# Third weight chunk loaded before the first gathers, half tile first in the last expert, two search waits lengthened: a retention and mixture-of-experts kernel on Trainium2

## The chip, the cores and the metric

The kernel runs on one core of one Trainium2 chip. The metric is device time in microseconds (us) of one execution; the medians below are over three executions. The engines of the core are TensorE (PE in the rows; its weight loads are PEld), VectorE (DVE), ScalarE (ACT), GpSimd (POOL) and SyncE (SP, which here only issues transfers). Each engine runs its own list of instructions in order, and waits on semaphores for the others.

## The reference

The first half is a retention layer: 8 batches, 8 heads, 576 positions, 64 elements a head. The second half is a mixture of 8 experts over the 4,608 tokens that result, with a strict routing: all (token, expert) scores are sorted, and a token goes to the best expert that still has one of its 576 places.

```python
scores = scale * np.matmul(q, k.transpose(0, 1, 3, 2))
ret = scores * Dmat[None, :, :, :]          # gamma**(i-j) where i >= j, else 0
x = np.matmul(ret, v)                       # -> N=4608 rows of D=512
logits = x @ w_gate                         # 4608 x 8
for idx in np.argsort(-logits.flatten()):
    tok, e = idx // E, idx % E
    if assigned[tok] >= 0 or counts[e] >= cap: continue
    assigned[tok] = e; counts[e] += 1
for e in range(E):
    h = np.maximum(x[assigned == e] @ w1[e], 0.0)      # 576x512 @ 512x1024
    out[assigned == e] = h @ w2[e]                     # 576x1024 @ 1024x512
```

All arrays are float32 in and out.

## The kernel before

**Stages.** `attention` (until about 140 us of the profile) streams 16 units of q, k and v through TensorE, writes the rows x to DRAM (`xd`) and forms the logits. Then the routing finds the experts one after the other: phase p finds the expert that fills up first among those left (a search over the bits of the scores, `search_first` for p = 0, `search` after that), its members (`members`), their row numbers (`listing`), and takes them out of the scores (`leave`). Phase 0 runs alone, from about 145 to 162 us, beside the last rows of x. Phases 1 to 7 are laid between the matrix products of the experts found before.

**One expert.** `l1` makes 16 tiles of the hidden layer (f = 0 to 7, each in two column groups s of 256 and 320 tokens), each from 12 products: every operand is split in a high and a low part (`xh`, `xl`, `w1h`, `w1l`), and three of the four combinations are multiplied. `l2` makes five tiles of the output, t = 0 to 3 with 128 tokens from 24 products each, t = 4 with the last 64 tokens from 16 products (it packs high and low parts beside each other, so that its two halves have to be added at the end). An expert has 192 + 112 = 304 products.

**Weights.** Each expert has eight chunks of 512 KB (four of w1, four of w2). `dma_pump` loads them on SP's queue into one of four `raw` buffers, and never more than `state['most']` in all until that is raised. `conv` turns one chunk into its high part (ACT, L946) and its low part: ACT writes the negated high part (L951) and a transfer issued by POOL adds the raw values (L952). For the first two chunks the low part of one is made by DVE (L949).

**The first expert.** When the first list is ready, `gather(0)` has POOL issue five indirect transfers of 128 rows (64 in the last) (L983). PE runs 25 empty products (`warm(25)`, L1175), then transposes the gathered rows (`pt`, L1015); ACT copies the high part `xh` out (L1017), DVE the low part `xl` (L1018). A tiny transfer `spacer2` on SP (L1144) waits for the third gather, so that SP's next weight loads start after it. In `l1` the first eight tiles are f = 0 to 3 with s = 0, then f = 0 to 3 with s = 1; the transpositions for j = 2, 3, 4 stand between tiles i = 2 to 4. With e == 0, f < 2 the order within a tile is all xh·w1h, then xh·w1l, then xl·w1h.

**What sets the order.** All of it is recorded in the program's order. A planner without knowledge of the chip (`Mixer`) lets a phase give up control with `yield (ns for DVE, ns for PE)`, and `mix.adv(ns)` after each group of products adds model time; when the model time of the yield has passed, the phase's next matmuls (L353 for the counts of a search step, L421 and L422 for the members, L459 and L462 for the list) are put behind the products recorded so far. From phase 2 on the model times of DVE are multiplied by 1.2 or 1.35. A larger number in a yield so puts the following PE instructions, and all that the phase does later, behind more products. On the chip each of those matmuls waits for DVE's result, and stands in line in front of the next product.

**The end.** After each `l2` tile ACT copies it to SBUF (L1109; L1111 and DVE's L1112 for t = 4), and POOL issues an indirect transfer to the output (L1069).

Of the kernel before, what the change touches and what calls it, by code (L numbers as in the profile page):

```python
# [15 lines left out]
AF = mybir.ActivationFunctionType  # L16
# [4 lines left out]
N, DM, E, FF = 4608, 512, 8, 1024  # L21
# [60 lines left out]
def rest(it):  # L82
    for _ in it:
        pass

class Route:
# [305 lines left out]
    def members(s, p):  # L392

        nc, V, pool, ps = s.nc, s.nc.vector, s.pool, s.ps
        mem = pool.tile([128, 2, 36], F32, name="mem")
        ba = pool.tile([128, 36], F32, name="ba")
        if p == E - 1:
            w = pool.tile([128, 8], F32, name="w8")
            V.tensor_scalar(w, s.nr, -10000.0, None, op0=ALU.is_ge)
            V.tensor_tensor(w, w, s.dec, op=ALU.mult)  # L400
            s.pick(w)
            V.tensor_scalar(ba, s.acc, s.mx, None, op0=ALU.is_equal)
            V.scalar_tensor_tensor(mem[:, 0], s.m, -1.0e38, ba, op0=ALU.is_ge, op1=ALU.add)
            V.memset(mem[:, 1], 0.0)
        else:
            V.scalar_tensor_tensor(mem, s.mx8[:, None, :].to_broadcast([128, 2, 36]), s.mx, s.ge, op0=ALU.is_equal, op1=ALU.mult)
            if p:
                V.scalar_tensor_tensor(mem[:, 0], s.acc, s.mx, mem[:, 0], op0=ALU.is_equal, op1=ALU.add)
        sc = pool.tile([128, 2, 36], BF16, name="sc")
        fl = lambda a: a.rearrange("p a b -> p (a b)")  # L410
        with nc.allow_low_precision(reason="counts up to 72"):
            V.tensor_tensor_scan(fl(sc), fl(mem), fl(mem), 0.0, op0=ALU.add, op1=ALU.bypass)

        sm = pool.tile([128, 2, 36], F32, name="sm")
        V.tensor_tensor(sm, sc, mem, op=ALU.mult)
        V.scalar_tensor_tensor(sm[:, 0], sm[:, 0], -1.0 - HALF, sm[:, 1], op0=ALU.add, op1=ALU.add)
        if not p:
            s.idle(6)
        yield (3000 if 0 < p < E - 1 else 1550 if not p else 1900), 125
        po = ps.tile([128, 2], F32, name="r")  # L420
        nc.tensor.matmul(po, s.tri, sc[:, :, 35], start=True, stop=False, skip_group_check=True)  # L421
        nc.tensor.matmul(po[:, 1:2], s.up, sc[:, 0, 35:36], start=False, stop=True, skip_group_check=True)  # L422
        q = pool.tile([128, 36], F32, name="pq")
        V.scalar_tensor_tensor(sm[:, 1], mem[:, 0], po[:, 0:1], sm[:, 0], op0=ALU.mult, op1=ALU.add)
        V.scalar_tensor_tensor(q, mem[:, 1], po[:, 1:2], sm[:, 1], op0=ALU.mult, op1=ALU.add)
        s.q, s.mem = q, mem
# [70 lines left out]
    def leave(s, p):  # L497

        nc, V, pool, ps = s.nc, s.nc.vector, s.pool, s.ps
        if p == 0:  # L500
            s.taken()
        e = pool.tile([128, 8], F32, name="eb")
        a = pool.tile([128, 36], F32, name="gone")
        V.tensor_scalar(e, s.es, -2*BIG, BIG, op0=ALU.mult, op1=ALU.add)
        V.scalar_tensor_tensor(a, s.q, CAP - HALF, s.mem[:, 1], op0=ALU.is_lt, op1=ALU.mult)
        V.tensor_tensor(s.Lg, s.Lg, e[:, None, :].to_broadcast([128, 36, 8]), op=ALU.min)
        V.tensor_tensor(a, a, s.gt, op=ALU.add)
        if p == 0:
            V.tensor_scalar(s.cap, a, -2*BIG, BIG, op0=ALU.mult, op1=ALU.add)
            V.tensor_tensor(s.acc, s.gt, s.mx8, op=ALU.mult)  # L510
        else:
            V.tensor_scalar(a, a, -2*BIG, BIG, op0=ALU.mult, op1=ALU.add)
            V.tensor_tensor(s.gt, s.gt, s.mx8, op=ALU.mult)
            V.tensor_tensor(s.cap, s.cap, a, op=ALU.min)
            V.tensor_tensor(s.acc, s.acc, s.gt, op=ALU.add)
        if p == 0:
            rest(s.best(capped=True))

            def after():
                cn = ps.tile([128, 8], F32, name="r")  # L520
                nc.tensor.matmul(cn, s.ones, s.n8, start=True, stop=True)
                s.room(cn)
            s.after = after
            yield 3800, 0
        else:
            rest(s.best(capped=True))
            yield (5000 if p == 1 else 4300), 0

def attention(tc, nc, P, qk, vk, cst_d, wg_d, rf, xd, Lg, raw):
    NC = cst_d.shape[1]  # L530
# [51 lines left out]
    def qscale(u, *parts):  # L582

        q, e = LD[u, 'q'], ex[:, u % HP]
        for a, b in parts:
            n = 128 if a < 1024 else 64
            x = q[:, a:b].rearrange("p (c i) -> p c i", i=n)
            nc.gpsimd.tensor_tensor(x, x, e[:, None, :n].to_broadcast([128, (b-a)//n, n]), op=ALU.mult)  # L588
# [205 lines left out]
    def fills(u, g):  # L794
        for f, a in fill.get(2*u + g, []): f(*a)

    P['warm'](7)
    qscale(0, (0, 512))
    kscale(0, 0, 8)
    scores(0, 0)  # L800
# [92 lines left out]
def moe(tc, nc, P, R, xd, w1_d, w2_d, out, mix):  # L893
    V, A, T = nc.vector, nc.scalar, nc.tensor
    ident, warm = P['ident'], P['warm']
# [1 line left out]
    ready = lambda k: len(found) > k  # L897
    regs, XG, quarters, parts = {}, {}, {}, {}
    xq = xd.rearrange("n (a c) -> (n a) c", a=4)
    state = dict(dma=0, conv=0, most=2, listing=-1)  # L900
    RAW, W1, W2, XH, XL = {}, {}, {}, {}, {}
    scat, lows = [], []
    spacer, spacer2 = [P['c'].tile([1, 1], F32, name=f"spacer{i}") for i in range(2)]
# [118 lines left out]
    def l1(e, tr):  # L1022

        hb = P['w'].tile([128, 8, 1152], F32R, name="hb", bufs=1)
        order = [(f, s) for f in range(8) for s in range(2)]
        if e == 0:
            order[:8] = [(f, s) for s in range(2) for f in range(4)]
        for i, (f, s) in enumerate(order):
            wh, wl = [w.rearrange("p (f d m) -> p f d m", f=2, d=4)[:, f % 2] for w in W1[e, f // 2]]
            if i == 0 and e >= PIECES:  # L1030
                for _ in tr:
                    pass
            if i == 0 and e:
                next(tr, None)
                next(tr, None)
            elif e == 0 and i in (2, 3):
                next(tr, None)
            elif i == (1 if e else 4):
                for _ in tr:
                    pass  # L1040
            xh, xl = XH[e], XL[e]
            c, n = ((slice(0, 256), 256), (slice(256, 576), 320))[s]

            ps = P['pp'].tile([128, n], F32, name="ph", tag="y" if f in (2, 5) else f"h{s}", bufs=2)
            terms = [(w[:, d], x[:, d, c]) for d in range(4) for w, x in ((wh, xh), (wh, xl), (wl, xh))]
            if e == 0 and f < 2:
                terms = terms[0::3] + terms[2::3] + terms[1::3]
            elif i in (2, 3) and e == 0:
                terms = terms[0::3] + terms[1::3] + terms[2::3]
            for k, (w, x) in enumerate(terms):  # L1050
                T.matmul(ps, w, x, start=(k == 0), stop=(k == 11))  # L1051
                if k % 3 == 2:
                    mix.adv(320 + 80*s, e == 0 and i < 3)
                    gather(e + 1)
            A.activation(hb[:, f, c], ps, AF.Relu)  # L1055
            for a, b in ((0, 256),) if s == 0 else ((0, 256), (256, 320)):
                to = (640 if a == 0 else 64) + 256*s
                V.scalar_tensor_tensor(hb[:, f, to+a:to+b], ps[:, a:b], 0.0, hb[:, f, 256*s+a:256*s+b].bitcast(F32),  # L1058
                                       op0=ALU.max, op1=ALU.subtract)
            mix.vec(340 + 140*s)  # L1060
            if e == 0 and i == 4:
                state['most'] = 8*E
            if i in ((2, 4, 7, 10) if e else (3, 5, 7, 9, 11, 13)):
                conv()
        return hb

# [8 lines left out]
    def l2(e, hb):  # L1075
# [1 line left out]
        late = []  # L1077
        want = 4*(e + 1 < E)
        wait = 0
        for t in range(5):  # L1080
            n = 128 if t < 4 else 64
            ps = P['pp'].tile([128, DM], F32, name="py", tag="y", bufs=2)
            c = slice(128*t, 128*t+n)
# [21 lines left out]
                    tr = transposes(e + 1)  # L1105
                next(tr, None)
            y = P['w'].tile([128, DM], F32, name="yt", bufs=3)
            if t < 4:
                A.activation(y, ps, AF.Copy)  # L1109
            else:  # L1110
                A.activation(y[:n], ps[n:], AF.Copy)  # L1111
                V.tensor_tensor(y[:n], y[:n], ps[:n], op=ALU.add)  # L1112
# [13 lines left out]
    def run():  # L1126
        mix.drain(lambda: 0 in regs)
        dma_pump()
        mix.drain(lambda: ready(0))
        conv(True)  # L1130
        conv()
        gather(0)
        lows.pop(0)()
        mix.step()
        warm(25)
        tr = transposes(0)
        next(tr)
        warm(4)
        next(tr)
        lows.pop(0)()  # L1140
        mix.step()
        warm(2)

        nc.sync.dma_start(spacer2, XG[0][0:1, 2, 0:1])  # L1144
        state['most'] = 4
        dma_pump()
        for e in range(E):
            tr = l2(e, l1(e, tr))
# [73 lines left out]
```

## Time and profile before

| | |
|---|---|
| three executions | 620.79, 623.42, 626.26 us; median 623.42 |
| the profiled execution | 625.75 us; span of the trace 623.6 us; 2.15 us lie around it |
| PE busy | 600.7 us, 96% |
| DVE, ACT, POOL busy | 66%, 44%, 40% |
[...]

All rows count microseconds from the start of the span. The time of an execution is the span and about 2 us more. The profiled execution is near the slowest of the three others.

### The profile page before, as it was taken

Reading aid. Unit: us, or ns where it says so; the run is one execution under the profiler, and the core shown is the slowest. Engines: PE = TensorE matmul, PEld = TensorE weight load, DVE = VectorE, ACT = ScalarE, POOL = GpSimd, SP = SyncE. Lnnn points to the kernel's source line nnn. Section 1 sums busy time; section 2 is a strip of 40 time slices with the busy share of each in tenths; the row PEclk is TensorE's granted clock in tenths of the full one; section 3 lists DMA queues with packets and bytes.
Section 4 is the critical chain, followed back from the end, with each engine's and each line's share of the span. In section 5 each row is a group of like instructions: output and inputs, shape, how many; then the busy total and the mean of one; then the engine's idle time right before and its main releaser. Section 6 shows DMA issues by size and latency. Waiting matters only on the chain.

```text
span 623.6 us, 14775 instructions
## 1 busy us (share of the span) xinstructions
PE 600.7 (96%) x5722; PEld 518.1 (83%) x5722; DVE 410.6 (66%) x1488; ACT 271.6 (44%) x465; POOL 248.2 (40%) x295
## 2 busy tenths in 40 slices
PE   7899999998989999999999999999999999999995
PEld 5788888875579779988987897799789889989983
DVE  4556788888868888887885877689478733322200
ACT  2244433333347355461652447155526445554410
POOL 4886665500302172061243242224313877832111
PEclk8899999999989999999999999999999999999998
DMA  9999899854768589787789399659937897994501
GB/s 330 408 369 401 280 370 316 261 140 137 192 180 194 174 221 264 186 207 236 156 224 246 94 229 227 201 111 231 247 114 174 200 245 169 259 249 124 102 35 42
DMA packets 53496, 133.22 MB, mean 214 GB/s; under 512 B 7410, under 2 KB 22642, under 8 KB 53426
## 3 DMA queue, kind: packets, MB, share of 16 engines
q0 software_dynamic: 15376, 51.92, 38.0%
q1 hardware_dynamic: 37906, 80.10, 38.0%
q8 instruction: 45, 0.74, 0.5%
q10 hardware_dynamic: 144, 0.26, 0.1%
q14 instruction: 25, 0.20, 0.1%
HBM read 80.35 MB, written 18.87 MB: 159 GB/s over the span
## 4 chain that ended last, share of the span: by engine, by line
PE 74%; DVE 9%; issue 6%; DMA 6%; POOL 2%; ACT 1%; SPq 1%; POOLq 0%; DVEq 0%
PE ph L1051 28%; PE py L1092 28%; PE sc L603 4%; PE px L647 3%; DMA xg<-xd,idx 2%; PE pS L624 2%; PE px L638 2%; PE pT L679 1%; DMA raw<-in_w 1%; PE r L353 1%; PE pt L1015 1%; DVE am L612 1%; DMA qin<-in_qk 1%; DVE cst L544 1%; DMA nin<-in_vk 1%
## 5 line engine op out<-in xcount | busy, mean ns | idle before, releaser
L1092 PE MATMUL py<-w2h,hb 128*128 128x512 f32 x576 | 187.3, 397 | 0.0
L1051 PE MATMUL ph<-xh,w1h 128*128 128x320 f32 (+1 forms) x512 | 151.7, 302 | 3.2 <-ACT xh L1017 3.2
L1051 PE MATMUL ph<-xh,w1l 128*128 128x320 f32 (+1 forms) x512 | 149.2, 297 | 0.0
L1051 PE MATMUL ph<-xl,w1h 128*128 128x320 f32 (+1 forms) x512 | 149.0, 297 | 0.0
L1092 PE MATMUL py<-w2l,hb 128*128 128x512 f32 (+1 forms) x320 | 125.3, 392 | 0.0
L1092 PEld LDWEIGHTS py<-w2h,hb 128*128 128x128 f32 x576 | 104.5, 188 | 21.7
L1051 PEld LDWEIGHTS ph<-xh,w1h 128*128 128x128 f32 x512 | 96.4, 191 | 4.4 <-ACT xh L1017 3.8
L1055 ACT ACTIVATE hb<-ph 128x256 fp32r<-128x256 f32 (+1 forms) x128 | 51.9, 408 | 105.1 <-PE ph L1051 96.3
L1051 PEld LDWEIGHTS ph<-xl,w1h 128*128 128x128 f32 x512 | 96.4, 191 | 0.3
L1051 PEld LDWEIGHTS ph<-xh,w1l 128*128 128x128 f32 x512 | 96.4, 191 | 0.0
L1058 DVE SCALAR_TENSOR_TENSOR hb<-ph,hb 128x256 fp32r<-128x256 f32 (+1 forms) x192 | 58.0, 352 | 46.2 <-ACT hb L1055 39.4
L1069 POOL DMA_INDIRECT out_y<-yt,idx x40 | 40.5, 1013 | 105.7 <-ACT yt L1109 70.5
L1092 PEld LDWEIGHTS py<-w2l,hb 128*128 128x128 f32 (+1 forms) x320 | 56.7, 177 | 12.9
L952 POOL DMA_DIRECT2D w2l<-raw x32 | 29.4, 919 | 87.2 <-ACT w2l L951 48.2
L612 DVE TENSOR_TENSOR am<-sc,cst 128x1024 f32<-128x1024 f32 x32 | 39.1, 1223 | 33.1 <-PE sc L603 33.0
L588 POOL TENSOR_TENSOR qin<-qin,cst 128x512 f32<-128x512 f32 (+1 forms) x48 | 48.3, 1034 | 31.2 <-DMA qin<-in_qk 27.3
L1109 ACT ACTIVATE yt<-py 128x512 f32<-128x512 f32 x32 | 19.2, 599 | 93.6 <-PE py L1092 70.0
L983 POOL DMA_INDIRECT xg<-xd,idx x30 | 30.2, 1008 | 71.9 <-DMA raw<-in_w 37.0
L627 ACT ACTIVATE st<-pS,cst 128x128 f32<-128x128 f32 x64 | 23.5, 368 | 79.9 <-PE pS L624 79.9
L952 POOL DMA_DIRECT2D w1l<-raw x31 | 29.0, 959 | 49.0 <-ACT w1l L951 32.5
L603 PE MATMUL sc<-qin,kin 64*128 64x128 f32 x512 | 38.8, 293 | 3.7 <-DVE am L612 1.9
L971 POOL DMA_INDIRECT xg<-xd,quarter x36 | 35.6, 989 | 12.8 <-issue 9.4
(191 smaller groups left out, 939.0 us busy)
## 6 DMA issues: line engine op xcount, KB each, us to landing
raw<-in_w SPq DMA_DIRECT2D x56, 512.0 KB
w2l<-raw POOLq DMA_DIRECT2D x32, 512.0 KB
w1l<-raw POOLq DMA_DIRECT2D x31, 512.0 KB
qin<-in_qk SPq DMA_DIRECT2D x14, 576.0 KB
kin<-in_qk SPq DMA_DIRECT2D x14, 576.0 KB
vin<-in_vk SPq DMA_DIRECT2D x14, 576.0 KB
nin<-in_vk SPq DMA_DIRECT2D x14, 512.0 KB
xd<-raw SPq DMA_DIRECT2D x36, 128.0 KB
```

Source lines behind the costliest of these rows:

```text
L588: nc.gpsimd.tensor_tensor(x, x, e[:, None, :n].to_broadcast([128, (b-a)//n, n]), op=ALU.mult)
L603: nc.tensor.matmul(t[:, h, 128*j:128*j+128], blk(k, 4*g+j)[r], blk(q, 4*g+j)[r], start=(j == 0), stop=True, skip_group_check=True)
L612: nc.vector.tensor_tensor(a, SC[u, g].rearrange("p h (j q) -> p h j q", q=128), m1[:, u % HP, :, None, :].to_broadcast([128, 2, 4, 128]), ...
L627: nc.scalar.activation(s, p, AF.Copy, scale=ss[:, u % HP, c:c+1])
L952: add = lambda: nc.gpsimd.dma_start(lo, raw, accum_op=ALU.add)
L971: nc.gpsimd.indirect_dma_start(out=t[:, k, :], out_offset=None, in_=xq[:, :], in_offset=bass.IndirectOffsetOnAxis(ap=quarters[e][:, v:v+1] ...
L983: nc.gpsimd.indirect_dma_start(out=xg[:n, j, :], out_offset=None, in_=xd[:, :], in_offset=bass.IndirectOffsetOnAxis(ap=found[e][:n, j:j+1] ...
L1051: T.matmul(ps, w, x, start=(k == 0), stop=(k == 11))
L1055: A.activation(hb[:, f, c], ps, AF.Relu)
L1058: V.scalar_tensor_tensor(hb[:, f, to+a:to+b], ps[:, a:b], 0.0, hb[:, f, 256*s+a:256*s+b].bitcast(F32), op0=ALU.max, op1=ALU.subtract)
L1069: st = nc.gpsimd.indirect_dma_start(out=out[:, :], out_offset=bass.IndirectOffsetOnAxis(ap=found[e][:n, t:t+1], axis=0), in_=y[:n], in_off ...
L1092: T.matmul(ps[:m], a, w, start=(k == 0), stop=(k == last), skip_group_check=True)
```

## The change

There are five edits. (1) `most` starts at 3, so that three weight chunks are loaded ahead of the gathers, and the third is converted in `run`, behind the second transposition, no longer inside `l1` at tile i = 3. (2) In the last expert (`e + 1 == E`) the half tile t = 4 is made first, and tile 3 last. (3) The copy of that last tile is split: 256 columns by ACT, 256 by DVE. (4) The yield of `members` for p = 1 goes from 3000 to 3500, and that of `leave` for p = 2 from 4300 to 5000 (times 1.2 in the planner). (5) At the very start PE runs 12 empty products where it ran 7.

```diff
-        yield (3000 if 0 < p < E - 1 else 1550 if not p else 1900), 125
+        yield (3500 if p == 1 else 3000 if 1 < p < E - 1 else 1550 if not p else 1900), 125
...
-            yield (5000 if p == 1 else 4300), 0
+            yield (5000 if p < 3 else 4300), 0
...
-    P['warm'](7)
+    P['warm'](12)
...
-    state = dict(dma=0, conv=0, most=2, listing=-1)
+    state = dict(dma=0, conv=0, most=3, listing=-1)
...
-            if i in ((2, 4, 7, 10) if e else (3, 5, 7, 9, 11, 13)):
+            if i in ((2, 4, 7, 10) if e else (5, 7, 9, 11, 13)):
                 conv()
...
-        for t in range(5):
+        for t in range(5) if e + 1 < E else (4, 0, 1, 2, 3):
...
-            if t < 4:
+            if t == 3 and e + 1 == E:
+                A.activation(y[:, :256], ps[:, :256], AF.Copy)
+                V.tensor_copy(y[:, 256:], ps[:, 256:])
+            elif t < 4:
                 A.activation(y, ps, AF.Copy)
...
         next(tr)
         lows.pop(0)()
+        conv()
         mix.step()
         warm(2)
```

ACT's list at the first expert, from the first two transposed row groups on, before (xh is the high part of the rows, hb the hidden layer; L946 and L951 convert a weight chunk):

```order
L951 ACTIVATE w1l<-raw 128x1024
L1017 ACTIVATE xh<-pt 128x4x128 x2
L1055 ACTIVATE hb<-ph 128x256 x2
L1017 ACTIVATE xh<-pt 128x4x128
L1055 ACTIVATE hb<-ph 128x256
L1017 ACTIVATE xh<-pt 128x4x128
L1055 ACTIVATE hb<-ph 128x256
L946 ACTIVATE w1h<-raw 128x1024
L951 ACTIVATE w1l<-raw 128x1024
L1017 ACTIVATE xh<-pt 128x4x64
```

and with the change:

```order
L951 ACTIVATE w1l<-raw 128x1024
L1017 ACTIVATE xh<-pt 128x4x128 x2
L946 ACTIVATE w1h<-raw 128x1024
L951 ACTIVATE w1l<-raw 128x1024
L1055 ACTIVATE hb<-ph 128x256 x2
L1017 ACTIVATE xh<-pt 128x4x128
L1055 ACTIVATE hb<-ph 128x256
L1017 ACTIVATE xh<-pt 128x4x128
L1055 ACTIVATE hb<-ph 128x256
L1017 ACTIVATE xh<-pt 128x4x64
```

The conversion of the third chunk no longer stands between the fourth hidden tile and the copy of the last transposed rows (128x4x64).

DVE's list at the same place, which is the same in both kernels; L357 to L348 are a step of the search of phase 1, xl is the low part of the last transposed rows, and the waits are in brackets:

```order
L357 SCALAR_TENSOR_TENSOR cs<-room,r 32x8 [waits PE_49]
L359 TENSOR_TENSOR cs<-cs,r 32x8 [waits DVE_49] x2
L361 TENSOR_TENSOR f<-r,cs 32x8 [waits DVE_49]
L361 TENSOR_TENSOR f<-r,cs 32x8 x3
L367 TENSOR_REDUCE mq<-f 128x1 [waits DVE_49]
L368 STREAM_TRANSPOSE tc<-mq 128x32 [waits DVE_49]
L369 TENSOR_REDUCE j<-tc 128x1 [waits DVE_49]
L337 TENSOR_SCALAR v<-u,j 128x72 [waits DVE_49]
L177 TENSOR_TENSOR G<-ct,v 128x1152 [waits DVE_49]
L348 TENSOR_TENSOR u<-v,D 128x36
L1058 SCALAR_TENSOR_TENSOR hb<-ph,hb 128x256 [waits Activation_49]
L1018 TENSOR_TENSOR xl<-pt,xh 128x4x64 [waits Activation_49]
```

Nothing moved here: the last low part stands behind the whole search step.

The end of the program, before: ACT's last copies, then DVE's last addition (DMASW names are earlier transfers of POOL):

```order
L1109 ACTIVATE yt<-py 128x512 [waits DMASW4_49,PE_49,Activation_49]
L1111 ACTIVATE yt<-py 64x512 [waits DMASW5_49,PE_49,Activation_49]
L1112 TENSOR_TENSOR yt<-yt,py 64x512 [waits DMASW5_49,DMASW6_49,DMASW1_49,Activation_49]
```

and with the change (L1114 and L1115 are the half tile, now the first of the five; L1109 and L1110 are the split copy):

```order
L1114 ACTIVATE yt<-py 64x512 [waits DMASW5_49,PE_49,Activation_49]
L1112 ACTIVATE yt<-py 128x512 [waits DMASW4_49,DVE_49,PE_49]
L1109 ACTIVATE yt<-py 128x256 [waits DMASW5_49,PE_49,Activation_49]
L1115 TENSOR_TENSOR yt<-yt,py 64x512 [waits DMASW5_49,Activation_49]
L1110 COPY yt<-py 128x256 [waits DMASW5_49,DMASW6_49,DMASW1_49,Activation_49]
```

Of the two halves of the last copy, ACT's waits for PE, and DVE's waits for ACT.

## Rows read from the trace of the kernel before

**Rows 1.** Page, part 1: busy time of each engine, share, instructions.

```profile
PE 600.7 (96%) x5722; PEld 518.1 (83%) x5722; DVE 410.6 (66%) x1488; ACT 271.6 (44%) x465; POOL 248.2 (40%) x295
```

**Rows 2.** Waits of PE: line waiting, releaser, us in total, times, longest.

```profile
PE ph L1051 <- ACT xh L1017: 3.2, 2, 3.0
...
PE sc L603 <- POOL qin L588: 1.7, 1, 1.7
```

**Rows 3.** Timeline, 172 to 183 us: start, duration, instruction, count, idle before.

```profile
175.01 0.14 DVE L357 SCALAR_TENSOR_TENSOR cs<-room,r 32x8 f32<-32x8 f32 x1
...
175.48 0.50 PE L1015 MATMUL pt<-ident,xg 64*128 64x64 f32 x4
...
176.68 1.06 ACT L946 ACTIVATE w1h<-raw 128x1024 fp32r<-128x1024 f32 x1 [0.70 <-DMA raw<-in_w]
...
178.17 0.42 DVE L1058 SCALAR_TENSOR_TENSOR hb<-ph,hb 128x256 fp32r<-128x256 f32 x1
178.58 0.36 ACT L1017 ACTIVATE xh<-pt 128x256 fp32r<-128x256 f32 x1
...
178.98 0.42 DVE L1018 TENSOR_TENSOR xl<-pt,xh 128x256 fp32r<-128x256 f32 x1 [0.39 <-ACT xh L1017]
179.00 1.44 PE L1051 MATMUL ph<-xh,w1h 128*128 128x320 f32 x4 [3.02 <-ACT xh L1017]
...
182.37 0.75 PE L1051 MATMUL ph<-xh,w1h 128*128 128x320 f32 x4
```

**Rows 4.** Stretches: us, busy time by engine, PEclk, DMA share, GB/s.

```profile
175.00:178.96 3.96, 0.98 (x9) 0.74 (x7) 3.25 (x15) 2.66 (x4) 0.00 (x0) 1.00 0.81 236
178.96:182.37 3.41, 3.37 (x13) 3.37 (x13) 0.42 (x1) 0.00 (x0) 0.99 (x1) 0.50 0.99 302
```

**Rows 5.** Stretches of 1 us before the first gathers move data.

```profile
160.00:161.00 1.00, 1.00 (x6) 0.44 (x5) 0.89 (x6) 0.00 (x0) 0.00 (x0) 1.00 0.95 381
...
162.00:163.00 1.00, 1.00 (x6) 0.49 (x5) 0.60 (x1) 0.93 (x2) 0.97 (x1) 1.00 0.00 0
```

**Rows 6.** Timeline, 157 to 168 us: SP's weight loads, ACT's second transposed copy.

```profile
157.08 0.89 SPq L932 DMA_DIRECT2D raw<-in_w  x2
...
167.60 0.60 ACT L1017 ACTIVATE xh<-pt 128x512 fp32r<-128x512 f32 x1 [0.92 <-PE r L521]
```

**Rows 7.** Timeline, the first 18 us.

```profile
1.48 3.17 PE L1175 MATMUL warm<-full 128*128 128x512 bf16 x7 [1.48 <-DVE full L1161]
...
14.77 1.69 POOL L588 TENSOR_TENSOR qin<-qin,cst 128x512 f32<-128x512 f32 x2 [1.67 <-DMA qin<-in_qk]
...
17.51 0.45 PE L624 MATMUL pS<-vin,ks 128*64 128x64 f32 x8 [2.07 <-POOL ks L593]
```

**Rows 8.** Timeline, 285 to 290 us: search of phase 3 at the half tile of the second expert.

```profile
286.49 0.39 PE L353 MATMUL r<-oh,G 128*128 128x32 bf16 x9
...
289.19 0.46 DVE L177 TENSOR_TENSOR G<-ct,v 128x576 bf16<-128x576 bf16 x1
...
289.71 0.39 PE L353 MATMUL r<-oh,G 128*128 128x32 bf16 x9 [0.41 <-DVE G L177]
```

**Rows 9.** Timeline, PE, 319 to 324 us: second transposition for the fourth expert.

```profile
321.61 0.53 PE L1015 MATMUL pt<-ident,xg 128*128 128x128 f32 x4 [0.23 <-DMA xg<-xd,idx]
```

**Rows 10.** Timeline, the last 12 us.

```profile
612.46 0.60 ACT L1109 ACTIVATE yt<-py 128x512 f32<-128x512 f32 x1 [4.89 <-PE py L1092]
...
613.34 0.97 POOL L1069 DMA_INDIRECT out_y<-yt,idx  x1 [4.24 <-ACT yt L1109]
...
615.68 0.40 PE L1092 MATMUL py<-w2l,hb 128*64 128x512 f32 x1
616.17 0.59 ACT L1111 ACTIVATE yt<-py 64x512 f32<-64x512 f32 x1 [3.11 <-PE py L1092]
616.79 0.68 DVE L1112 TENSOR_TENSOR yt<-yt,py 64x512 f32<-64x512 f32 x1 [25.14 <-ACT yt L1111]
617.75 0.90 POOL L1069 DMA_INDIRECT out_y<-yt,idx  x1 [3.35 <-DVE yt L1112]
```

## The prediction, before the changed kernel was run

> **What bounds the kernel now.** I read the page's busy shares first. TensorE is busy for 600.7 of 623.6 us [rows 1], so all idle time of PE together is 23 us. About 7.5 of them lie behind its last product (616.08 to the end), so no edit that leaves the products alone can win much. The second view is the list of PE's waits: the only large one is 3.0 us for `xh`, the high part of gathered rows [rows 2]. The third is the timeline around it [rows 3]. PE ends the last transposition of the first expert at 175.98 (175.48 + 0.50) and starts the next tile at 179.00. Between them ACT stands at a weight conversion: it waits for the third chunk until 176.68, converts it in two passes, and only then copies the transposed rows (178.58 to 178.94). [...]
>
> **The third chunk, step by step.** The edit takes the conversion out of that place on ACT and puts it behind the second transposed copy, which ends at 168.20 [rows 6]. There it takes about 2.1 us (two passes of 1.06 [rows 3]), to 170.3. The first tile's twelve products start about 168.2 and take at most 0.14 each, so its copy comes some 0.4 us late; nobody waits for it, since DVE is in a search step and PE's next tiles have banks of their own. The third load goes out behind the two of 157.08 [rows 6]. It moves 0.52 MB, which at the 381 GB/s of the stretch from 160 takes 1.4 us, and from 162 to 163 the transfer engines carry nothing, while POOL is still issuing the first gather [rows 5]. So I price it at nothing, with the whole 1.4 us as the upper end.
>
> The last transposed copy then follows PE at once: 175.98 + 0.06 + 0.36 gives 176.4, and PE starts at 176.5 instead of 179.00. But what is late next is on DVE. Its list has not moved: the low part `xl` stands behind a whole search step that began at 175.01 and behind a hidden tile that ends at 178.59 (178.17 + 0.42); before, it waited another 0.39 for ACT. It will run from 178.6 to 179.0 [rows 3]. Eight of the tile's products need no `xl`: 8 x 0.14 brings PE to 177.6, there it waits 1.4 us, and the last four end at 179.6. Before, the tile ended at 182.37 [rows 3]. So the three microseconds are not all won: of 3.02 idle 1.9 remain, in pieces of 0.5 and 1.4. What is won depends on the clock. If it stays at its full level, the gain is 182.37 - 179.6 = **2.7 us**. If it falls at the same time, four products take 1.1 and PE is then eight products ahead at 182.37, **1.0 us** at full speed. The nearest rows are two pauses in the first 18 us, of 1.7 [rows 2] and 2.1 us [rows 7] in one piece, and 3.0 us here. I take 2.7, because the work between the two pieces parts them, and keep 1.0 as the other end. All further steps of phase 1 move with PE, as their products do.
>
> **The end.** Before, from the last product's end (615.68 + 0.40 = 616.08): ACT from 616.17 for 0.59, DVE from 616.79 for 0.68, POOL from 617.75 [rows 10]: 1.67 us to the issue. With the change the last tile is a full one, in two copies of 256 columns. The order shows DVE's half waiting for ACT's, so they run one after the other: 0.09, then 0.38 for ACT (by its 0.36 for 128x256 [rows 3]), 0.03, then 0.42 for DVE (its 128x256 rows [rows 3]), 0.28 to POOL: 1.20. The issue of 128 rows takes 0.97 against 0.90 [rows 10]. The gain is **0.4 us**. Twice the bytes in the last transfer could cost up to 0.34 us (128 KB at 381 GB/s), and halves side by side would give 0.8: ends 0 and 0.8. A single copy of 512 columns by ACT takes 0.60 [rows 10] and would end 0.2 us sooner than the two. [...]
>
> The half tile first costs nothing: its sixteen products use the last hidden tile only in the last two, 14 x 0.23 = 3.2 us behind the last product of `l1`, and the copies of such a tile (0.36 and 0.42 for 256 columns, [rows 3]) are done well before.
>
> **The later search steps.** Only the step at 289.71 waited, 0.41 us [rows 8]. It had ten products of 0.23 behind the step at 286.49, and needed 3.16 (to 289.65). Counting the lists, this interval now has 22 products, but the one before it, between third and fourth count, shrinks from 15 to 12, all half-tile products. They give 2.81 + 2 x 0.23 = 3.27, and the wider comparison (128x1152, up to twice 0.46) needs 3.2 to 3.6: a wait of 0 to 0.35. I take 0.2, a gain of 0.2. Against it, the list of phase 3 is now ready 18 products later, and the transpositions that need its rows only 9. The way between them loses 18 hidden products (2.5 us) and gains 9 output products (2.1). The second of those transpositions already waited 0.23 for its gather [rows 9]; it will wait 0.6. Net **+0.2 us**, ends -0.6 and +0.8. The weight loads of that expert start later by the same 18 products, and their first conversion comes only with the output tiles, so I count nothing else as late.
>
> **The twelve empty products at the start.** Seven run from 1.48 to 4.65 [rows 7], and PE then waits 1.7 us for the first scaled q [rows 2]. Five more at 0.45 end at 6.9, up to 0.5 us behind the 6.37 at which it went on. Whatever is won or lost there meets the next bound: at 14.77 POOL waits for q from DRAM, and PE waits for POOL until 17.51 [rows 7]. I take **0**; ends +0.5, and -0.7 if the clock of a later scores tile rises.
>
> **Sum.** -2.7 - 0.4 + 0.2 + 0 = -2.9 us on the profiled execution's own 625.75, so 622.9. That execution lies 2.3 us above the median of three, 623.42; the same 2.9 taken from the median gives **620.5 us**.
>
> **The rivals.**
> - *The clock falls again.* Two pauses of 1.9 us in all are about as long as the ones that it followed in the first 18 us. Then the term is 1.0, the sum -1.2: 622.2 us. For it: those rows. Against it: they were in one piece. Chance 0.28.
> - *Slower: the third load holds up the gathers.* If it still moves when they start, the first transposition comes up to 1.4 us late, and every tile behind it. A longer pause there can bring the clock down as well, 1.7 us. With the smaller gain at the old place: 1.4 + 1.7 - 1.2 = +1.9, so 625.3. It decides once the gathers lose more than 1.2 us. Against it: the empty microsecond in rows 5. [...] Chance 0.07.
> - *The change does little.* DVE's chain is later than I have it, or the runs that make the median had no fall of the clock, so that there is only a pause to shorten: 0.5 us at most is left after the +0.2 and noise, 623. Chance 0.12.
> - *The start counts.* The clock stays up from the first scores on, and 1 us of it reaches the end: 619.5. Chance 0.10.
>
> **The numbers.** My forecast, 620.5, has 0.43. Its own range is 619 to 622. The three executions before differ by 5.5 us, so a median of few can be off by 2 by itself. A range from 617.8 to 624.0 takes in all cases but the slower one and the tails. About 1% (6.2 us) is what a measurement of this kernel can tell from no change. To be faster by that, all idle at the first expert and a good part of the start would have to go: 0.07. Slower by over 1% needs the gathers' mishap and more: 0.03. Within 1%: 0.90.
>
> **What would show it.** In the changed profile PE's wait for ACT `xh` of 3.0 should be about 0.5, and a wait for DVE `xl` (L1018) of about 1.4 should stand in its place; if that is missing, my reading of DVE's list is wrong. The granted clock behind it tells forecast from first rival. The first gather should be issued about 1 us after the list as before, and the first transposition wait no more than 0.3 longer; if not, the second rival. At the end DVE's copy should start after ACT's ends, and the issue come 1.2 us behind the last product. Around the half tile of the second expert a wait of 0.2, and one of about 0.6 for the gather of the fourth. If the time is under 617, I have missed something at the start or in the clock.

## The result, and the profile after

The change made the kernel **slower by half a per cent to 0.8 per cent**: the median of 19 runs is 627.07 us (621.13 to 633.61), against 622.13 us (619.87 to 626.26) for the kernel before, 4.9 us more; the ratio estimated from the runs is 1.0055, 95% interval 1.0035 to 1.0076. Ratios, and the differences that I draw, leave disturbed runs out: two of the change's 19 (the median of the others is 627.03), and one of twelve of a kernel below with a median of 625.15 us (624.61 without it). I had forecast 620.5 us, range 617.8 to 624.0.

The execution profiled for the kernel after took 621.13 us, the lowest of its 19 runs, and its span was 619.2 us; its mean granted TensorE clock was 0.998 of full speed (0.988 in the profiled execution before). So its profile shows what the edits did, but not what an execution usually costs; a second profile stands among the experiments. PE's part of the busy shares, and the largest waits of PE (columns as in [rows 2]), are:

```profile
PE 597.8 (97%) x5723; PEld 514.5 (83%) x5727; DVE 406.0 (66%) x1489; ACT 271.8 (44%) x465; POOL 248.0 (40%) x295
```

```profile
PE pS L624 <- POOL ks L593: 2.9, 1, 2.9
PE ph L1051 <- ACT xh L1001: 1.7, 1, 1.7
...
PE ph L1051 <- DVE xl L1018: 1.1, 1, 1.1
PE sc L603 <- POOL qin L588: 0.9, 2, 0.6
PE ph L1051 <- ACT xh L1017: 0.7, 2, 0.5
```

The 3.0 us wait for L1017 of [rows 2] is down to 0.5, and the new 1.1 us for `xl` is the one that I had expected. Two lines I had not expected: 2.9 us for the scaled keys `ks` in the first 20 us (2.07 before [rows 7]), and 1.7 us for an `xh` of another line, L1001. That line belongs to the last two experts. Their rows (e >= PIECES, which is 6) are not gathered by five transfers but by 18 transfers of quarter rows, which POOL issues one by one (L971) between its other transfers; DVE transposes them (L999), ACT copies the high part (L1001), DVE the low part (L1002).

The first expert, timeline of after (columns as in [rows 3]):

```profile
172.04 0.50 PE L1015 MATMUL pt<-ident,xg 64*128 64x64 f32 x4
...
172.58 0.38 ACT L1017 ACTIVATE xh<-pt 128x256 fp32r<-128x256 f32 x1
...
173.01 0.85 PE L1051 MATMUL ph<-xh,w1h 128*128 128x320 f32 x4 [0.47 <-ACT xh L1017]
...
175.07 0.41 DVE L1018 TENSOR_TENSOR xl<-pt,xh 128x256 fp32r<-128x256 f32 x1
...
176.24 0.30 PE L1051 MATMUL ph<-xh,w1h 128*128 128x320 f32 x1
```

From the last transposition's end to the next tile it now takes 176.24 - 172.54 = 3.70 us, against 182.37 - 175.98 = 6.39 in [rows 3]: 2.69 less, where I had put 2.7. The end, timeline of after:

```profile
611.68 0.39 PE L1092 MATMUL py<-w2l,hb 128*128 128x512 f32 x1
612.15 0.38 ACT L1109 ACTIVATE yt<-py 128x256 f32<-128x256 f32 x1 [4.89 <-PE py L1092]
612.57 0.42 DVE L1110 COPY yt<-py 128x256 f32<-128x256 f32 x1 [20.89 <-ACT yt L1109]
613.27 0.97 POOL L1069 DMA_INDIRECT out_y<-yt,idx  x1 [4.67 <-DVE yt L1110]
```

From the last product's end (612.07) to the issue it is 1.20 us, as forecast, against 1.67 in [rows 10]. So the two edits on which my sum rested did what I had said; the loss is elsewhere.

### The profile page after: what moved, and what is told of

The parts are those of the page before. It is cut to its first block, busy times and chain, and to the rows that moved or that the text cites. A ratio compares the mean times of both kernels' runs of the same rounds, so it can differ in the third digit from the quotient of the medians.

```text
span 619.2 us, 14782 instructions
## 1 busy us (share of the span) xinstructions
PE 597.8 (97%) x5723; PEld 514.5 (83%) x5727; DVE 406.0 (66%) x1489; ACT 271.8 (44%) x465; POOL 248.0 (40%) x295
## 4 chain that ended last, share of the span: by engine, by line
PE 74%; issue 7%; DMA 6%; DVE 6%; POOL 4%; ACT 1%; SPq 1%; POOLq 0%; DVEq 0%
PE ph L1051 31%; PE py L1092 24%; PE sc L603 4%; PE px L647 3%; PE px L638 2%; PE pS L624 2%; POOL xg L971 2%; PE r L353 2%; PE pt L1015 1%; PE pT L679 1%; DMA w2l<-raw 1%; DVE am L612 1%; DMA qin<-in_qk 1%; DMA nin<-in_vk 1%; DMA xg<-xd,quarter 1%
## 5 line engine op out<-in xcount | busy, mean ns | idle before, releaser
L1092 PEld LDWEIGHTS py<-w2h,hb 128*128 128x128 f32 x576 | 104.6, 188 | 21.9
L952 POOL DMA_DIRECT2D w2l<-raw x32 | 29.2, 914 | 85.5 <-ACT w2l L951 50.3
L612 DVE TENSOR_TENSOR am<-sc,cst 128x1024 f32<-128x1024 f32 x32 | 39.1, 1221 | 34.1 <-PE sc L603 34.1
L1112 ACT ACTIVATE yt<-py 128x512 f32<-128x512 f32 x31 | 18.5, 597 | 87.6 <-PE py L1092 60.5
L952 POOL DMA_DIRECT2D w1l<-raw x31 | 28.9, 945 | 42.5 <-ACT w1l L951 34.9
L971 POOL DMA_INDIRECT xg<-xd,quarter x36 | 35.9, 997 | 14.0 <-issue 9.1
L603 PE MATMUL sc<-qin,kin 64*128 64x128 f32 x512 | 37.2, 285 | 1.1 <-POOL qin L588 0.9
```

Of the source, the lines that this page charges most:

```text
L603: nc.tensor.matmul(t[:, h, 128*j:128*j+128], blk(k, 4*g+j)[r], blk(q, 4*g+j)[r], start=(j == 0), stop=True, skip_group_check=True)
L612: nc.vector.tensor_tensor(a, SC[u, g].rearrange("p h (j q) -> p h j q", q=128), m1[:, u % HP, :, None, :].to_broadcast([128, 2, 4, 128]), ...
L952: add = lambda: nc.gpsimd.dma_start(lo, raw, accum_op=ALU.add)
L971: nc.gpsimd.indirect_dma_start(out=t[:, k, :], out_offset=None, in_=xq[:, :], in_offset=bass.IndirectOffsetOnAxis(ap=quarters[e][:, v:v+1] ...
L1092: T.matmul(ps[:m], a, w, start=(k == 0), stop=(k == last), skip_group_check=True)
```

## Experiments

Three theories at the start. **S**: the later search steps put the lists of the last phases later, and POOL's pieces for the seventh expert with them; alone they should cost 3 to 6 us, with a wait of 1 to 3 us at that expert's second tile. **W** (rival): the five further empty products at the start cost the time. **G** (rival): the third chunk's load or conversion does. The first kernels do one part alone or leave one out.

**The search steps alone** (before, with)

```
-        yield (3000 if 0 < p < E - 1 else 1550 ...), 125
+        yield (3500 if p == 1 else 3000 if 1 < p < E - 1 else 1550 ...), 125
-            yield (5000 if p == 1 else 4300), 0
+            yield (5000 if p < 3 else 4300), 0
```

> The kernel before with the two later search steps alone (3500 products' worth behind the first count of phase 1, 5000 behind phase 2). [...] Theory W, the five further empty products at the start are the loss: same as before within 1 us. Theory G, the third chunk's load or conversion is the loss: same as before within 1 us.

Measured 626.56 us, ratio 1.0054 (1.0027 to 1.0082). S holds in size, 3.5 us above the 623.02 of the kernel before. In place it was a miss: this profile shows no wait for L1001, but one of 2.0 us for a list matmul, in phase 7, which came late because DVE stood still for 3.9 us ahead of one step:

```profile
490.60 0.26 DVE L424 SCALAR_TENSOR_TENSOR sm<-mem,r,sm 128x36 f32<-128x36 f32 x1 [3.90 <-PE py L1092]
```

```profile
493.91 0.84 PE L459 MATMUL r<-rh,G 128*128 128x160 bf16 x9 [1.96 <-DVE rh L453]
```

The product that the profile names is not one that this step needs; I saw that pause in no other profile, and its cause stays open. It held PE up, and in this execution the last piece for the seventh expert is transposed at 514.44, ahead of the expert's first product (514.93). So this run shows what the steps cost, but not where.

**The third chunk alone** (before, with)

```
-    state = dict(dma=0, conv=0, most=2, listing=-1)
+    state = dict(dma=0, conv=0, most=3, listing=-1)
-            if i in ((2, 4, 7, 10) if e else (3, 5, 7, 9, 11, 13)):
+            if i in ((2, 4, 7, 10) if e else (5, 7, 9, 11, 13)):
         lows.pop(0)()
+        conv()
```

> The kernel before with the third weight chunk alone. Theory S: the wait of 3.0 us for xh goes to 0.5 and 1.1 as in the change, no wait of the seventh expert for its pieces, and the time is 0.5 to 2.5 us below before. Theory G: the load meets the gathers or the conversion delays others, and the time is 3 to 6 us above before. Theory W: 0.5 to 2.5 us below before, as by S.

Measured 620.53 us, ratio 0.9953 (0.9929 to 0.9977): 2.5 us below the 623.02 of the kernel before, measured beside it. G falls.

**The empty products alone** (before, with `P['warm'](12)` for `P['warm'](7)`)

> The kernel before with twelve empty products at the start in place of seven, alone. Theory W: the clock's course from the start on changes and the time is 3 to 6 us above before. Theories S and G: within 0.7 us of before, since the scores wait for q from DRAM at 14 us all the same.

Measured 629.28 us, six runs, ratio 1.0100 (1.0064 to 1.0136). W holds as well: it and S are both true, and I had set them up as rivals.

**The change without the search steps** (3000 and 4300 as before)

> The changed kernel with the two search steps back at 3000 and 4300. Theory S: the wait of the seventh expert for its gathered pieces goes, and the time is 1 to 3 us below before, 4 to 8 below the change. Theories W and G: the time stays where the change has it, 3 to 6 us above before.

Measured 625.15 us, ratio 1.0011 (0.9980 to 1.0041): 2.4 us below the change (624.61 against 627.03), not 4 to 8. W's part is still in it.

**Seven empty products, the rest of the change** (`P['warm'](7)`)

> The changed kernel with seven empty products at the start again, so third chunk, end and later search steps together. If the first four runs add up (chunk -2.5 us, steps +3.5 us, end -0.4 us), it comes to about 0.6 us above before, with the pieces of the seventh expert late as in the change. If the steps cost nothing once TensorE is earlier at the first expert (the rival), about 620, 3 us below before.

Measured 624.51 us, ratio 1.0019 (0.9994 to 1.0044): 1.4 us above the 623.14 of before, where the parts gave 0.6. They add up to within a microsecond, and the rival falls. PE waits 3.5 us for L1001 in its profile.

**Third chunk and the end alone**

> Third chunk and the last expert's edits alone: seven empty products, search steps as before. By the prediction's term for the end 0.4 us less than the chunk alone (620.5), about 620.1 and 2.9 us below before. Rival: the half tile first needs the last chunk of the second weights sooner (a wait of 0.4 us for w2l stands in the changed profile) and takes the gain back, 620.5 to 621.

Measured 619.95 us, ratio 0.9955 (0.9927 to 0.9983). With the steps it is 624.51: the steps cost 4.6 us here. Against the chunk alone the end's 0.4 us is too little to tell by time; the rows of the tail are its evidence.

**The lists of the last two phases back at their old places** (seven empty products, and)

```
-            yield (5000 if p < 3 else 4300), 0
+            yield (5000 if p < 3 else 3800 if p == 5 else 4300), 0
```

> The changed kernel with seven empty products and with the yield behind phase 5 at 3800 in place of 4300: the lists of the phases 6 and 7 are then behind 1625 and 1739 products, exactly as before, while those of the phases 1 to 5 stay as late as in the change. Theory S6, only the seventh expert's pieces cost: no wait for them, and 3 to 4 us below the kernel with seven empty products and the change's steps, at about 620. Rival, what is late in the phases 3 to 5 costs too (about 0.8 us in the fourth expert of the profile): 1 to 2 us above that.

Measured 619.79 us, ratio 0.9938 (0.9910 to 0.9966): 4.7 below the kernel that differs from it by this number alone. S stands, and only the lists of the last two phases count: with those of the phases 1 to 5 still late, the time is that of the kernel with none late (619.95). The timelines of POOL, DVE, ACT and PE show how. First with 4300 (the kernel of 624.51 us); the seventh expert's first product is at 508.69:

```profile
475.75 1.07 POOL L971 DMA_INDIRECT xg<-xd,quarter  x1 [3.38 <-DVE eb L504]
...
504.47 1.03 POOL L952 DMA_DIRECT2D w1l<-raw  x1
505.80 1.06 POOL L971 DMA_INDIRECT xg<-xd,quarter  x1 [0.30 <-issue]
...
512.84 0.45 DVE L999 STREAM_TRANSPOSE xz<-xg 128x256 f32<-128x256 f32 x1 [4.81 <-DMA xg<-xd,quarter]
513.32 0.42 ACT L1001 ACTIVATE xh<-xz 128x256 fp32r<-128x256 f32 x1 [5.20 <-DVE xz L999]
...
513.79 0.41 PE L1051 MATMUL ph<-xh,w1h 128*128 128x320 f32 x1 [3.52 <-ACT xh L1001]
```

Then with 3800 behind phase 5 (the expert's first product is at 507.16):

```profile
473.04 1.07 POOL L971 DMA_INDIRECT xg<-xd,quarter  x1 [2.20 <-DVE eb L504]
...
502.57 0.95 POOL L971 DMA_INDIRECT xg<-xd,quarter  x1 [0.30 <-issue]
...
503.52 1.03 POOL L952 DMA_DIRECT2D w1l<-raw  x1
...
507.18 0.45 DVE L999 STREAM_TRANSPOSE xz<-xg 128x256 f32<-128x256 f32 x1 [2.99 <-DMA xg<-xd,quarter]
...
507.66 0.42 ACT L1001 ACTIVATE xh<-xz 128x256 fp32r<-128x256 f32 x1 [2.89 <-DVE xz L999]
...
508.59 0.31 PE L1051 MATMUL ph<-xh,w1h 128*128 128x320 f32 x1
```

Counted from the expert's first product, the first piece is issued 32.9 us ahead with 4300 instead of 34.1 with 3800, because the list is behind 1631 products instead of 1625. The eighteenth piece is issued 2.9 us ahead instead of 4.6: the 1.2 us, and part of another issue, for with 4300 it stands behind a transfer for the weights (L952) that it is ahead of with 3800. It is also used later: 7.0 us from issue to DVE's transposition instead of 4.6. The second tile then waits 3.5 us. What follows, in stretches of that kernel (columns as in [rows 4]):

```profile
510.20:513.70 3.50, 0.07 (x1) 0.00 (x0) 0.86 (x2) 0.38 (x1) 0.00 (x0) 1.00 0.91 344
514.20:517.60 3.40, 3.35 (x14) 3.35 (x14) 1.01 (x2) 0.55 (x3) 1.89 (x2) 0.51 0.19 43
517.70:521.10 3.40, 3.40 (x28) 3.40 (x27) 0.98 (x3) 2.30 (x4) 1.91 (x2) 1.00 0.24 63
```

After 3.5 us with hardly a product the granted clock is 0.51, and 14 products take the 3.4 us in which 28 go behind them, at 1.00. The pause of 3.5 and half of 3.4 make 5.2 us; the two medians differ by 4.7.

**The pause at the start filled** (third chunk, end, twelve empty products, old search steps, and ten empty products ahead of the third tile of scores)

```
             if n <= last:
+                if u == 0 and g:
+                    fl = P['pp'].tile([128, 2, 512], F32, name="sc", tag="sc")
+                    for _ in range(10):
+                        nc.tensor.matmul(fl[:, 0], P['full'][:, :128], P['full'], start=True, stop=True)
                 scores(n, m)
```

> Third chunk, end and twelve empty products at the start, search steps as before, and ten more empty products ahead of the third tile of scores, where TensorE otherwise waits 3 us for the scaled keys. Theory P, the pause of 3 us brings the granted clock down just when the data are there: the pause goes to under 1 us, the falls of the clock between 16 and 23 us go, and the time is 619 to 621, 4 to 6 below the same kernel without the filling (625.15). Rival, the early products in themselves or what they do to the transfers cost the time: 625 or more.

Measured 621.90 us, ratio 0.9966 (0.9944 to 0.9987): 2.7 us below the kernel without the filling (624.61). Theory P holds for most of the cost, which is 4.7 by 619.95 us with seven empty products. In the timeline of PE, first the kernel of 619.95 us (seven empty products), then that of 625.15 us (twelve), then this one:

```profile
11.08 2.08 PE L603 MATMUL sc<-qin,kin 64*128 64x128 f32 x16
...
17.07 1.16 PE L603 MATMUL sc<-qin,kin 64*128 64x128 f32 x16
18.16 0.45 PE L624 MATMUL pS<-vin,ks 128*64 128x64 f32 x8
```

```profile
13.56 1.16 PE L603 MATMUL sc<-qin,kin 64*128 64x128 f32 x16 [0.17 <-POOL qin L588]
17.91 0.70 PE L624 MATMUL pS<-vin,ks 128*64 128x64 f32 x8 [3.19 <-POOL ks L593]
```

```profile
15.73 1.16 PE L603 MATMUL sc<-qin,kin 64*128 64x128 f32 x16
17.38 0.45 PE L624 MATMUL pS<-vin,ks 128*64 128x64 f32 x8 [0.48 <-POOL ks L593]
```

With seven empty products the second tile of scores takes 2.08 us, nearly twice the 1.16 of the third (the granted clock shows 1.00 from 9 to 13 us; the products' length tells more). TensorE is slow while it would wait for data anyway, reaches the keys at 18.16 without a wait, and is fast from then on (77 products at 1.00 in the 3.4 us from 16.2). With twelve it is fast from the first tile (1.16 us), runs out of data, waits 3.2 us in one piece, and is slow just when the data are there: 24 products from 16 to 20 us, at a granted clock of 0.53.

**Both repairs together** (twelve empty products with the ten more, and 3800 behind phase 5)

> The changed kernel with both losses taken out in their own ways: twelve empty products stay and ten more fill the pause ahead of the third tile of scores, and the yield behind phase 5 is 3800. If the two causes are the whole of the loss, 618 to 620.5, no slower than with seven empty products (619.8). If the early start keeps a cost of its own beside the pause (621.9 with the filling against 619.95 without early products), about 621.5.

Measured 621.44 us, ratio 0.9976 (0.9948 to 1.0004). It is the second of the two cases: with the early start the median stays 1.7 us higher, here (621.44 against 619.79) as with the old search steps (2.0: 621.90 against 619.95). The runs overlap widely (618.50 to 624.23 here, 617.86 to 621.85 there), so that this rest is not shown beyond the noise. In the profiles it does not lie in the attention: the last tile of scores starts at 127.48 with the pause filled and at 127.18 with seven empty products. Where it goes, if it is real, is open.

**One copy at the end** (the kernel of 619.79 us, last tile copied by ACT alone; one run, 620.90 us)

> The kernel with seven empty products and 3800 behind phase 5, with the last tile copied by ScalarE in one piece of 512 columns. By the prediction's sum for the end: 0.09 + 0.60 + 0.28 = 0.97 us from the last product's end to POOL's issue, against 1.20 with the two halves one after the other. Rival: the issue waits for something else, and it stays at 1.2.

```profile
611.56 0.39 PE L1092 MATMUL py<-w2l,hb 128*128 128x512 f32 x1
612.04 0.60 ACT L1109 ACTIVATE yt<-py 128x512 f32<-128x512 f32 x1 [4.89 <-PE py L1092]
612.91 0.97 POOL L1069 DMA_INDIRECT out_y<-yt,idx  x1 [4.43 <-ACT yt L1109]
```

From the last product's end (611.95) to the issue it is 0.96 us. By these rows the split of the last copy loses 0.24 us.

**The change once more**

> The changed kernel once more, for a second profile. If its usual time near 627 comes from the two pauses, the profile shows the granted clock at 0.50 behind one or both of them (16 to 23 us; behind the wait of the seventh expert near 510 us), and 624 to 629 us. If it shows no such fall and yet 626 or more, the cause is another.

It took 629.37 us, just above the range. PE's two largest waits, and the stretches behind them:

```profile
PE ph L1051 <- ACT xh L1001: 3.6, 1, 3.6
PE pS L624 <- POOL ks L593: 3.2, 1, 3.2
```

```profile
16.20:19.60 3.40, 2.16 (x24) 2.17 (x26) 0.00 (x0) 0.37 (x1) 3.34 (x4) 0.50 1.02 412
19.60:23.10 3.50, 3.50 (x45) 3.05 (x43) 0.00 (x0) 0.96 (x2) 3.50 (x5) 0.51 1.02 409
23.10:26.50 3.40, 3.40 (x76) 2.97 (x74) 3.19 (x4) 1.22 (x3) 2.74 (x4) 1.00 1.03 404
```

```profile
518.00:521.40 3.40, 3.40 (x13) 3.40 (x14) 1.01 (x2) 0.56 (x3) 1.89 (x2) 0.50 0.21 52
```

Both pauses are there, both followed by a granted clock of 0.50: the two causes in one execution. The execution profiled first had both pauses, shorter, and no such clock behind either. After 2.9 us at the start and 1.7 us near 509 it stayed at 1.00:

```profile
19.60:23.10 3.50, 3.50 (x76) 3.04 (x68) 2.13 (x3) 1.65 (x5) 3.50 (x5) 1.00 1.03 413
...
510.80:514.20 3.40, 3.35 (x23) 3.13 (x24) 1.96 (x6) 1.38 (x3) 1.55 (x2) 1.00 0.73 267
```

The length of a pause alone does not part the two: in the profile of before the pauses of 1.7 and 2.1 us were followed by 0.51 (8.4 to 11.8 us) and 0.50 (18.5 to 21.9). What decides is not shown.

What the slow stretch at the start grows into, in the timeline of PE: the fifth tile of scores in the kernel of 619.95 us, then in the change once more, with two later tiles that wait for `am`, DVE's masked scores.

```profile
23.93 1.16 PE L603 MATMUL sc<-qin,kin 64*128 64x128 f32 x16
```

```profile
25.77 1.16 PE L603 MATMUL sc<-qin,kin 64*128 64x128 f32 x16
...
37.34 1.16 PE L603 MATMUL sc<-qin,kin 64*128 64x128 f32 x16 [1.19 <-DVE am L612]
...
76.07 1.16 PE L603 MATMUL sc<-qin,kin 64*128 64x128 f32 x16 [1.00 <-DVE am L612]
```

The profile of 619.95 us has no such wait. In the first profile of the change, with the pause but without the slow clock behind it, the fifth tile starts at 23.43, no later than in the six profiles with seven empty products that begin slowly (23.42 to 23.98). So by these rows it is the slow stretch behind the pause that costs, and not the pause itself.

## Why the prediction was wrong, point by point

- **Third chunk: right.** 2.69 us in the rows for 2.7, the wait for `xl` 1.1 for 1.4, and -2.5 us by the run that had this edit alone. That its 620.53 us is the number that I forecast for the whole is chance. The rival with the clock also occurs: of ten profiles of kernels with the third chunk, at least three have a slow stretch right behind this place (granted clock 0.57 from 176 to 180 us with the third chunk alone, 0.57 from 180 to 184 without the search steps; with the pause filled four products took 1.43 us at 177.36, and 0.86 at the same place in the first profile of the change). The 1.1 us for four products and the 1.7 us of the forecast's slow cases are my estimates from [rows 3] and [rows 4], twelve products in 3.37 us at 0.50, half of that at 1.00; the runs show the same products every 0.27 us at 0.50 (518.37 to 518.91 in the second profile of the change) and every 0.15 at 1.00 (508.59 to 509.04 with 3800 behind phase 5). A gather of the first expert kept PE waiting for 1.2 us in one of the ten (the filled pause, 621.90 us), by 0.3 at most in the others: the rival of the held-up gathers is rare.
- **The end: right** by the rows, 1.20 us and 0.96 for one copy where I had 0.97. The times cannot show the 0.4 us.
- **The later search steps: this step failed.** I priced them at +0.2 us from the search of phase 3 and the fourth expert's gather, and wrote "so I count nothing else as late". For these two places it was near: a wait of 0.3 for DVE's `G` where I had 0.2, none for the gather where I had 0.6. But the shift goes on to the last phases: the lists of phases 3 to 6 came 18, 15, 9 and 6 products later. Six products, at the first of the two experts whose rows come in 18 pieces, cost 4.6 us. With the lists at their old places ACT's copy of the last rows ends at 508.08, and the second tile starts at 508.59: there was half a microsecond to give. (The eighth expert's last rows are copied 13.0 us ahead of its second tile in the profile of before, and 13.9 in that of after.) I had not looked there, since PE did not wait.
- **The twelve empty products: this step failed too.** I took 0, ends +0.5 and -0.7, because "whatever is won or lost there meets the next bound" at 14.77. The bound was real: TensorE got the third tile's keys at 17.2 to 17.9 us in all profiles with twelve, 17.51 before [rows 7]. What I left out is that a TensorE which comes sooner to a fixed bound waits longer there, 2.9 to 3.2 us in one piece in the four profiles with twelve and no filling, and that a slow clock can then follow with the data there: a mean of 0.50 to 0.57 in three of the four, within 16 to 20 us. Cost: 624.61 against 619.95, 4.7 us. The last product of the scores starts at 128.1 in the profile of the latter and at 133.5 in the second profile of the change. Of these 5.4 us, 1.8 are there at the fifth tile, and 2.2 come in the two waits for `am` at 37 and 76 us; why DVE is late there is open.
- **A row that misled me.** The profiled execution of before has its first tile of scores fast (1.16 us), and a pause of 2.1 us, followed by a granted clock of 0.50 from 18.5 to 21.9. The other six profiles with seven empty products begin slowly, with 2.08 us for that tile, and wait at most 1.1 us there. I took an unusual start as the kernel's own.
- **The rivals.** "Slower", with a chance of 0.07 for the gathers of the first expert, was the right side by the wrong mechanism; no rival had the gathers of the last ones. The chance of 0.90 for within 1% covers the result; the range did not, since I bounded both failed terms too tightly.
- **What is not settled.** Alone, the steps cost 3.5 us and the empty products 6.3, and the chunk wins 2.5 and the end 0.4: 6.9 in all, where the change has 4.9 by the medians and 3.4 (2.2 to 4.7) by the ratio. The empty products alone have six runs (4.0 to 8.5 us), so that this may be noise. With the empty products the steps cost 2.4 us (3.3 when each kernel is counted from the kernel before, measured beside it), without them 4.6. Whether the two causes really take less together is open.

## What to carry to other kernels

A step that is moved later in a hand-laid order moves all that hangs on it, to the end of the program: follow the shift to the place with the least slack, which is a wait of an engine other than the bound one, and read the slack there. Before waking TensorE up earlier, ask where its next data come from: here a transfer set that time, and a slow TensorE in front of it (2.08 us for a tile) still came to the keys without a wait at 18.16, where a fast one (1.16) paid for its pause of 3.2 us with a granted clock of 0.53 just when the data came. Ask more than one execution for a start that can go two ways.

## What I had not expected of the hardware

- A pause of 3.5 us and the slow stretch behind it come to 5.2 us by the rows (4.7 by the medians): 14 products in the 3.4 us behind it, at a granted clock of 0.51, where 28 went in the next 3.4, at 1.00.
- A pause of 2.9 us at the start, without such a stretch (the granted clock stayed at 1.00), cost nothing there: the fifth tile of scores started at 23.43, against 23.42 to 23.98 in six profiles with seven empty products.
- Ten products that compute nothing, put into a wait of 3.2 us, won 2.7 us.
- The eighteenth piece took 7.0 us from issue to DVE's use behind a weight transfer, and 4.6 ahead of it.
